# The pooled probabilities of batches 1 to 3, normalised block by block on ScalarE instead of at once on GpSimd

## The chip, the core and the metric

The kernel is one program on one core of a Trainium2 chip. A core has a matrix engine (TensorE, in the profile PE, its weight loads PEld), a vector engine (VectorE, DVE), an engine for functions and scaled copies (ScalarE, ACT), a general engine (GpSimd, POOL) that here also issues the accumulating DMAs, and SyncE (SP), which issues the other DMAs. Each engine runs its instructions strictly in order; semaphores tie the engines together. The metric is device time in microseconds, the median of three runs.

## The reference, cut to what matters

Three layers follow each other: an attention with a pooled and a local part, a channel mix, and a gated convolution. The part that the change touches is the softmax of the pooled attention.

```python
def sm_attn(qq, kk, vv):
    s = scale * np.matmul(qq, kk.transpose(0, 1, 3, 2))
    s = s - np.max(s, axis=-1, keepdims=True)
    a = np.exp(s)
    a = a / (np.sum(a, axis=-1, keepdims=True) + 1e-09)
    return np.matmul(a, vv)
q_d = q.reshape(B, H, Sd, factor, D).mean(axis=3)     # k_d, v_d likewise; Sd = 144
out_up = np.repeat(sm_attn(q_d, k_d, v_d), factor, axis=2)
...                                                   # out_local: 7 keys around each query
x = (out_up + out_local)                              # 4 batches, 8 heads of 64, 576 positions
x = _moe_ref(x, mu_k, mu_r, w_k, w_v, w_r)            # squared-relu channel mix, 512 -> 1024 -> 512
return _moe2_ref(x, w_in, conv_w, w_out)              # gate, 3-tap convolution, 512 -> 1024 -> 512
```

## The kernel before, in words

The attention of a batch is done for two groups of four heads (gp 0 and 1). A group consists of steps, each a function that issues a few instructions on one engine: the local scores (TensorE L504 and L513, then VectorE L530, L531, L542, L548 and ScalarE L539), the pooled scores (TensorE L575, 32 queries by 144 keys, so that 128 partitions hold a block of four heads and five blocks hold all queries), their softmax, then the way out: `down_out` transposes the pooled probabilities (L639), copies the transposes to SBUF on ScalarE (L647), multiplies by the pooled v (L662), copies again (L674, L676); `local_out` transposes the local probabilities (L694), copies (L699), multiplies (L713) and VectorE adds both parts (L728).

The pooled softmax runs like this: VectorE finds the maxima (L591, L592), ScalarE takes five exponentials with their sums (L598, one per block of 128 by 144), VectorE inverts the sums (L484, L485), and one engine multiplies the tile `pd` of 128 by 720 by the inverted sums (L610). For batch 0 that engine is VectorE, for batches 1 to 3 GpSimd: six instructions, one for each group of heads.

The channel mix of the batch before runs between these steps on TensorE: `up` (L869, L808 for the very first half batch) and `down` (L918, L836), in units of 12 matmuls (4 fp32 ones for L808 and L836). ScalarE and VectorE cut the weights, which arrive as fp64, into fp32 and then into two fp32r parts (L379, L380, L361, L364, L400 or L402, L406), and the activations likewise (L776 to L792, L888 to L906). The last third of the program is the gated convolution.

The order of each engine's instructions is not written by hand. `Program.order` is a list planner: every step has an engine (or a choice of engines), an estimated length and a list of keys that it reads and writes; from the back it works out a latest start for each step, shifted by a table of numbers per step (`EARLY`), and then fills the engines in planned time, each taking the ready step with the earliest latest start. Steps that may run on VectorE or ScalarE go to the one that the plan has free. A changed engine or length of one step therefore moves other steps as well, on every engine.

Of the kernel before, what the change touches and what calls it, by code (L numbers as in the profile page):

```python
# [14 lines left out]
AF = mybir.ActivationFunctionType  # L15
# [53 lines left out]
class Program:  # L69
# [15 lines left out]
    def step(self, engine, us, f, r=(), w=(), due=None, slack=1.0):  # L85
        n = len(self.steps)
        deps = set()
        for k in r:
            if k in self.writer:
                deps.add(self.writer[k])  # L90
        for k in w:
            deps.update(self.readers.pop(k, ()))
            if k in self.writer:
                deps.add(self.writer[k])
        for k in r:
            self.readers.setdefault(k, set()).add(n)
        for k in w:
            self.writer[k] = n
        deps.discard(n)
        self.steps.append((engine, us, f, due, slack))  # L100
        self.tags.append(self.tag)
        self.deps.append(deps)
        return n
# [95 lines left out]
def dve(n):  # L199
    return 0.13 + 1.1e-3 * n  # L200
# [19 lines left out]
def tile_local_attention__then__channel_mix__then__conv_glu(  # L220
# [16 lines left out]
    nc = tc.nc  # L237
# [8 lines left out]
    SD = S // FAC  # L246
# [11 lines left out]
    scale = 1.0 / math.sqrt(D)  # L258
# [82 lines left out]
    def ring(name, tiles, one=0):  # L341

        i = count[name] = count.get(name, -1) + 1
        i %= one or len(tiles)
        return tiles[i], (name, i)
# [68 lines left out]
    def group(b, gp):  # L414
# [7 lines left out]
        def tag(kind, i0):  # L422
            prog.tag = kind, b, gp, i0
# [58 lines left out]
        def inverse(rs, guard_scale):  # L482

            nc.vector.tensor_scalar(rs, rs, 1e-9, guard_scale, op0=ALU.add, op1=ALU.mult)  # L484
            nc.vector.reciprocal(rs, rs)  # L485
# [68 lines left out]
        def down_blocks(i0, i1):  # L554
            q0, m = i0 * PB, (i1 - i0) * PB
            qs = [min(q, q0 + m - BQ) for q in range(q0, q0 + m, BQ)]
            return q0, m, qs

        def down_scores(i0, i1):
            tag("ds", i0)  # L560
            q0, m, qs = down_blocks(i0, i1)
            nq = len(qs)
            pst, pk = ring("a2", a2_t)
            pd, pdk = ring("pd", pd_t, int(b > 0))
            sm, smk = ring("sums", sums)
            g["pd", i0] = (pd, pdk)
            mx, rs = sm[:, 0, 0:nq], sm[:, 1, 0:nq]
            sc = scale / FAC ** 2
            def f():
                for c in range(0, nq, 2):  # L570
                    for h in range(4):
                        for r in range(min(2, nq - c)):
                            q, at = qs[c + r], h ^ r
                            d, rows = g["kqd"][0][:, h // 2], slice(h % 2 * D, (h % 2 + 1) * D)
                            nc.tensor.matmul(  # L575
                                pst[at * BQ:(at + 1) * BQ, r, c // 2 * SD:(c // 2 + 1) * SD],
                                lhsT=d[rows, SD + q:SD + q + BQ], rhs=d[rows, 0:SD], start=True, stop=True,
                            )

            step(  # L580
                "PE", 0.2 * nq, f,
                [(g["kqd"][1], i, pr) for i in {0, i0} for pr in range(2)],
                [(pk, 0), (pk, 1)], slack=SL[i0 > 0],
            )
            for r in range(2):
                n_r = len(range(r, nq, 2))
                pv = pst[:, r, 0:n_r * SD].rearrange("p (c s) -> p c s", s=SD)

                def top(r=r, pv=pv):
                    m = mx[:, r:nq:2]  # L590
                    nc.vector.reduce_max(m, pv, axis=AX.X)  # L591
                    nc.vector.tensor_scalar_mul(m, m, -sc)  # L592

                step("DVE", 0.33 + 1.1e-3 * n_r * SD, top, [(pk, r)], [(smk, r)], slack=SL[i0 > 0])

                def ex(r=r, pv=pv):
                    for c in range(r, nq, 2):
                        nc.scalar.activation(  # L598
                            pd[:, c], pv[:, c // 2], AF.Exp, bias=mx[:, c:c + 1], scale=sc,
                            accum_out=rs[:, c:c + 1],  # L600
                        )

                step("ACT", 0.37 * n_r, ex, [(smk, r)], [(pk, r), (smk, "r", r), (pdk, r)], slack=SL[i0 > 0])
            step(
                "DVE", 0.4, lambda: inverse(rs, FAC), (), [(smk, "r", r) for r in range(2)], slack=SL[i0 > 0],
            )
            engine, us = ("DVE", dve) if b == 0 else ("POOL", pool)

            def norm(eng):
                eng.tensor_tensor(  # L610
                    out=pd[:, 0:nq], in0=pd[:, 0:nq], in1=rs.unsqueeze(2).to_broadcast([P, nq, SD]), op=ALU.mult
                )

            step(
                (engine,), (us(nq * SD),), norm, [(smk, "r", r) for r in range(2)],
                [(pdk, r) for r in range(2)], slack=SL[i0 > 0],
            )

# [61 lines left out]
        def local_out(i0, i1):  # L680
# [24 lines left out]
            for pr, hp in enumerate(pairs):  # L705
# [30 lines left out]
                step("DVE", 0.8, add, [odk], [(pk, 0), (pk, 1)] + ks, slack=SL[i0 > 0])  # L736

        return {"loads": loads, "kqd": pooled_kq, "s": local_scores, "ds": down_scores,
                "do": down_out, "lo": local_out}

# [663 lines left out]
```

## Time and profile before

| | |
|---|---|
| median of 3 runs | 584.84 us (584.05 to 585.73) |
| span of the profiled execution | 584.2 us, mean granted TensorE clock 0.991 |
| TensorE busy | 553.3 us (95%), weight loads 510.7 us |
| VectorE busy | 380.5 us (65%) |
| ScalarE busy | 329.3 us (56%) |
| GpSimd busy | 52.0 us (9%) |

The span runs from the first to the last instruction of one execution that the profiler recorded; the page gives no other time for that execution. A line of a timeline gives the start, the length from the first start to the last end of instructions of one form that follow each other, their number, and in brackets the idle time before them with what ended it. Instructions of one engine overlap at their edges, so that two starts are often closer than one length.

### The profile page before, as it was taken

Reading aid. Unit: us, or ns where it says so; the run is one execution under the profiler, and the core shown is the slowest. Engines: PE = TensorE matmul, PEld = TensorE weight load, DVE = VectorE, ACT = ScalarE, POOL = GpSimd, SP = SyncE. Lnnn points to the kernel's source line nnn. Section 1 sums busy time; section 2 is a strip of 40 time slices with the busy share of each in tenths; the row PEclk is TensorE's granted clock in tenths of the full one; section 3 lists DMA queues with packets and bytes.
Section 4 is the critical chain, followed back from the end, with each engine's and each line's share of the span. In section 5 each row is a group of like instructions: output and inputs, shape, how many; then the busy total and the mean of one; then the engine's idle time right before and its main releaser. Section 6 shows DMA issues by size and latency. Waiting matters only on the chain.

```text
span 584.2 us, 14308 instructions
## 1 busy us (share of the span) xinstructions
PE 553.3 (95%) x5900; PEld 510.7 (87%) x5900; DVE 380.5 (65%) x795; ACT 329.3 (56%) x779; POOL 52.0 (9%) x133
## 2 busy tenths in 40 slices
PE   4579979899999999999999999999999999999996
PEld 3457758789999999999999999899899898998995
DVE  6787698688534355344925899587586686395580
ACT  2458678576646475455838865455454455363441
POOL 3002021021121312110000000000000000000000
PEclk9999989898999999999999999999999999999999
DMA  9858998869467576712530530310400400100101
GB/s 262 292 191 216 296 293 209 283 181 302 141 136 207 113 220 160 171 51 76 187 116 2 202 110 0 123 42 0 146 18 1 145 19 1 54 2 1 54 2 54
DMA packets 42449, 74.14 MB, mean 127 GB/s; under 512 B 3648, under 2 KB 28736, under 8 KB 41472
## 3 DMA queue, kind: packets, MB, share of 16 engines
q1 hardware_dynamic: 38064, 65.27, 33.7%
q0 software_dynamic: 4320, 7.97, 8.9%
q8 instruction: 46, 0.75, 0.5%
q14 instruction: 19, 0.16, 0.1%
HBM read 59.06 MB, written 14.16 MB: 125 GB/s over the span
## 4 chain that ended last, share of the span: by engine, by line
PE 82%; DVE 7%; DMA 5%; ACT 3%; issue 2%; SPq 1%; ACTq 0%; POOL 0%; DVEq 0%
PE a L1301 17%; PE mm L869 15%; PE mm L918 15%; PE a L1221 8%; PE mm L1221 7%; PE mm L1180 4%; PE a L1180 4%; PE a L713 3%; DMA st_d<-in_moe_w_k 2%; DMA st_d<-in_moe_w_v 2%; PE a L694 2%; PE mm L836 2%; PE mm L808 1%; PE a L513 1%; PE a L639 1%
## 5 line engine op out<-in xcount | busy, mean ns | idle before, releaser
L1301 PE MATMUL a<-wk,wv 128*128 128x512 f32 x432 | 100.9, 390 | 0.0
L918 PE MATMUL mm<-k,wv 128*128 128x288 f32 x672 | 97.4, 301 | 0.2 <-ACT tmp L888 0.2
L1301 PEld LDWEIGHTS a<-wk,wv 128*128 128x128 f32 x432 | 80.9, 188 | 15.8
L869 PE MATMUL mm<-xk,wk 128*128 128x288 f32 x672 | 94.6, 299 | 0.0
L918 PEld LDWEIGHTS mm<-k,wv 128*128 128x128 f32 x672 | 91.9, 191 | 0.8 <-ACT tmp L888 0.5
L869 PEld LDWEIGHTS mm<-xk,wk 128*128 128x128 f32 x672 | 91.1, 191 | 1.1 <-issue 0.5
L1221 PE MATMUL mm<-k,wi 128*128 128x386 f32 x288 | 53.2, 338 | 0.4 <-ACT k L1205 0.3
L1221 PE MATMUL a<-k,wi 128*128 128x386 f32 x288 | 53.1, 338 | 0.0
L906 DVE TENSOR_TENSOR k<-tmp,k 128x288 fp32r<-128x288 f32 x56 | 25.7, 464 | 41.9 <-ACT k L899 41.2
L1221 PEld LDWEIGHTS mm<-k,wi 128*128 128x128 f32 x288 | 50.7, 188 | 1.5 <-ACT k L1205 0.7
L1221 PEld LDWEIGHTS a<-k,wi 128*128 128x128 f32 x288 | 50.8, 188 | 0.2
L728 DVE TENSOR_TENSOR xT<-a,od 128x288 f32<-128x288 f32 (+2 forms) x40 | 13.8, 392 | 37.6 <-PE a L713 37.6
L1276 ACT ACTIVATE tmp<-tmp 128x384 f32<-128x384 f32 x48 | 25.1, 523 | 21.6 <-DVE tmp L1270 21.6
L1266 DVE TENSOR_SCALAR tmp<-h,cw_sb 128x384 f32<-128x384 f32 x48 | 20.0, 417 | 25.6 <-ACT h L1251 12.2
L888 ACT ACTIVATE tmp<-mm 128x288 f32<-128x288 f32 x56 | 23.0, 412 | 22.3 <-PE mm L869 22.1
L1270 DVE SCALAR_TENSOR_TENSOR tmp<-h,cw_sb,tmp 128x384 f32<-128x384 f32 x48 | 29.7, 619 | 2.6
L1267 DVE SCALAR_TENSOR_TENSOR tmp<-h,cw_sb,tmp 128x384 f32<-128x384 f32 x48 | 29.7, 619 | 2.3
L1316 ACT ACTIVATE xT<-a 128x512 f32<-128x512 f32 x18 | 10.3, 597 | 36.2 <-PE a L1301 34.4
L1286 ACT CAST wv<-tmp 128x384 fp32r<-128x384 f32 x48 | 24.1, 511 | 9.3 <-DVE tmp L1279 9.2
L1279 DVE SCALAR_TENSOR_TENSOR tmp<-tmp,h 128x384 f32<-128x384 f32 x48 | 25.9, 553 | 3.0 <-ACT tmp L1276 2.5
L1288 DVE TENSOR_TENSOR wv<-tmp,wv 128x384 fp32r<-128x384 f32 x48 | 25.7, 553 | 2.9 <-ACT wv L1286 2.3
L361 DVE SCALAR_TENSOR_TENSOR st_f<-st_f,st_d 128x512 uint32<-128x512 uint32 x28 | 20.3, 725 | 11.1 <-ACT st_d L380 10.8
(149 smaller groups left out, 889.1 us busy)
## 6 DMA issues: line engine op xcount, KB each, us to landing
kq<-in_kq SPq DMA_DIRECT2D x12, 576.0 KB, 5.0
vw<-in_vw SPq DMA_DIRECT2D x6, 1152.0 KB, 9.5
kqd<-in_kqp POOLq DMA_DIRECT2D x18, 288.0 KB, 5.5
x_d<-xT SPq DMA_DIRECT2D x16, 288.0 KB, 7.0
v_d<-tmp SPq DMA_DIRECT2D x32, 144.0 KB, 4.0
out_dram<-xT SPq DMA_DIRECT2D x18, 256.0 KB, 2.0
st_d<-in_moe_w_k SPq DMA_DIRECT2D x8, 512.0 KB, 4.5
st_d<-in_moe_w_v SPq DMA_DIRECT2D x8, 512.0 KB, 5.4
```

The lines of the kernel that those rows point to most:

```text
L869: nc.tensor.matmul(pst[:, 0:NH], lhsT=wk_t[wt][:, kt, mt * P:(mt + 1) * P], rhs=xk[:, xs, kt, :], start=(kt == 0 and g == 0), stop=(kt == ...
L906: ("DVE",), (dve(NH),), lambda e, r=r, kh=kh, kl=kl: e.tensor_sub(kl, r, kh.bitcast(F32)),
L918: nc.tensor.matmul(pst[:, 0:NH], lhsT=wv_t[wt][:, kt, mt * P:(mt + 1) * P], rhs=xs, start=(kt == 0 and g == 0), stop=(kt == KF - 1 and g = ...
L1180: nc.tensor.matmul(pst[:, 0:CW], lhsT=late["wr"][wt][:, kt, mt * P:(mt + 1) * P], rhs=r_t[xs][:, kt, :], start=(kt == 0 and g == 0), stop= ...
L1221: nc.tensor.matmul(pst[:, 0:CW], lhsT=late["wi%d" % (mt * P // HF)][wt][:, kt, mt * P % HF:mt * P % HF + P], rhs=x1s[xs][:, kt, :], start= ...
L1267: nc.vector.scalar_tensor_tensor(out=cv, in0=tap(0), scalar=cw[:, 0, mt:mt + 1], in1=cv, op0=ALU.mult, op1=ALU.add)
L1270: nc.vector.scalar_tensor_tensor(out=cv, in0=tap(2), scalar=cw[:, 2, mt:mt + 1], in1=cv, op0=ALU.mult, op1=ALU.add)
L1276: step("ACT", act(CH), lambda: nc.scalar.activation(cv, cv, AF.Tanh, scale=0.5), (), [cvk])
L1279: lambda: nc.vector.scalar_tensor_tensor(out=gt, in0=cv, scalar=1.0, in1=tap(1), op0=ALU.add, op1=ALU.mult),
L1286: step("ACT", act(CH), lambda: nc.scalar.copy(gh, gf), ["wv_old", gk], [("gh", j)])
L1288: ("DVE",), (0.56,), lambda e: e.tensor_sub(gl, gf, gh.bitcast(F32)),
L1301: nc.tensor.matmul(pst, lhsT=xs[:, tt * P:(tt + 1) * P], rhs=wo[wt][:, kt, :], start=(kt == 0 and g == 0), stop=(kt == KF - 1 and g == 2),)
```

## The change

The planner's step for the normalisation of batches 1 to 3 is given to ScalarE with an estimated length of 0.3 us per block; the step issues five ACTIVATE instructions (Copy, scale taken per partition from the inverted sums of that block), where GpSimd issued one multiplication.

```diff
@@ -604,15 +604,19 @@
             step(
                 "DVE", 0.4, lambda: inverse(rs, FAC), (), [(smk, "r", r) for r in range(2)], slack=SL[i0 > 0],
             )
-            engine, us = ("DVE", dve) if b == 0 else ("POOL", pool)
+            engine, us = ("DVE", dve(nq * SD)) if b == 0 else ("ACT", 0.3 * nq)
 
             def norm(eng):
+                if eng is nc.scalar:
+                    for c in range(nq):
+                        eng.activation(pd[:, c], pd[:, c], AF.Copy, scale=rs[:, c:c + 1])
+                    return
                 eng.tensor_tensor(
                     out=pd[:, 0:nq], in0=pd[:, 0:nq], in1=rs.unsqueeze(2).to_broadcast([P, nq, SD]), op=ALU.mult
                 )
 
             step(
-                (engine,), (us(nq * SD),), norm, [(smk, "r", r) for r in range(2)],
+                (engine,), (us,), norm, [(smk, "r", r) for r in range(2)],
                 [(pdk, r) for r in range(2)], slack=SL[i0 > 0],
             )
 
```

Line numbers behind the change are larger by 4 (L639 is L643, L647 is L651, L662 is L666, L694 is L698, L713 is L717, L836 is L840, L853 is L857, L869 is L873, L918 is L922).

The planner's order changes from the first of the six normalisations on. On ScalarE, at batch 1, group 0, before (`pd` the pooled probabilities, `probs` the local ones, `pdt` the transposed pooled ones, `st_d` and `st_f` weights as loaded and as fp32, `mm` the sums of the channel mix in PSUM):

```order
L598 ACTIVATE pd_142,sums_148<-a_161,sums_148 128x144 x5
L379 ACTIVATE st_f_113<-st_d_110 128x512
L380 ACTIVATE st_d_110<-st_d_110 128x512
L400 CAST wv_117<-st_ff_152 128x4x128
L379 ACTIVATE st_f_114<-st_d_111 128x512
L380 ACTIVATE st_d_111<-st_d_111 128x512
L853 COPY tmp<-mm_156 128x288
L400 CAST wv_117<-st_f_113 128x4x128
L539 ACTIVATE probs_139<-probs_139 128x18x38
L647 COPY pdt_144<-a_158 72x2x128
L647 COPY pdt_144<-a_160 72x2x512
L853 COPY tmp<-mm_157 128x288
```

and now:

```order
L598 ACTIVATE pd_142,sums_148<-a_161,sums_148 128x144 x5
L379 ACTIVATE st_f_113<-st_d_110 128x512
L380 ACTIVATE st_d_110<-st_d_110 128x512
L400 CAST wv_117<-st_ff_152 128x4x128
L612 ACTIVATE pd_142<-pd_142,sums_148 128x144 x5
L379 ACTIVATE st_f_114<-st_d_111 128x512
L380 ACTIVATE st_d_111<-st_d_111 128x512
L539 ACTIVATE probs_139<-probs_139 128x18x38
L651 COPY pdt_144<-a_160 72x2x512
L651 COPY pdt_144<-a_158 72x2x128
L857 COPY tmp<-mm_156 128x288
L857 COPY tmp<-mm_157 128x288
```

The five scaled copies stand behind the cast that was there; the exponential of the local scores and the two copies of `pdt` now stand ahead of the two copies out of `mm`, and the cast of `st_f_113` has left ScalarE.

On TensorE in the same place, from the transposes of `pd` on, before:

```order
L639 MATMUL a_158<-ident,pd_142 72x128 x2
L639 MATMUL a_160<-ident,pd_142 72x128 x8
L836 MATMUL mm_156<-xT_120,st_f_113 128x288 x4
L662 MATMUL a_159<-pdt_144,vd_137 64x3x32 x4
L662 MATMUL a_159<-pdt_144,vd_137 64x2x32 x4
L662 MATMUL a_159<-pdt_144,vd_137 64x3x32 x4
L662 MATMUL a_159<-pdt_144,vd_137 64x2x32 x4
L694 MATMUL a_158<-ident,probs_139 128x128 x4
L836 MATMUL mm_156<-xT_120,st_f_114 128x288 x4
```

and now:

```order
L643 MATMUL a_158<-ident,pd_142 72x128 x2
L643 MATMUL a_160<-ident,pd_142 72x128 x8
L666 MATMUL a_159<-pdt_144,vd_137 64x3x32 x4
L666 MATMUL a_159<-pdt_144,vd_137 64x2x32 x4
L666 MATMUL a_159<-pdt_144,vd_137 64x3x32 x4
L666 MATMUL a_159<-pdt_144,vd_137 64x2x32 x4
L840 MATMUL mm_156<-xT_120,st_f_113 128x288 x4
L698 MATMUL a_158<-ident,probs_139 128x128 x4
L698 MATMUL a_159<-ident,probs_139 128x128 x4
L840 MATMUL mm_157<-xT_120,st_ff_151 128x288 x4
L698 MATMUL a_158<-ident,probs_139 128x128
L840 MATMUL mm_156<-xT_120,st_f_114 128x288 x4
```

The multiplication by the pooled v (L662, now L666) has moved ahead of the unit of the channel mix (L836, now L840) that stood between it and the transposes, and the local multiplication (L717) stands ahead of the last unit of L840.

On TensorE at the local scores of batch 2, group 0 (`a_160`, each run of L513 has eight rows in its second half), before:

```order
L513 MATMUL a_160<-kq_130 32x38 x4
L918 MATMUL mm_157<-k_123,wv_117 128x288
...
L869 MATMUL mm_156<-xk_122,wk_115 128x288
...
L575 MATMUL a_161<-kqd_133 32x144 x20
L513 MATMUL a_160<-kq_129 32x38 x4
L513 MATMUL a_160<-kq_130 32x38 x4
...
L918 MATMUL mm_156<-k_123,wv_117 128x288
```

and now:

```order
L513 MATMUL a_160<-kq_130 32x38 x4
L922 MATMUL mm_156<-k_123,wv_117 128x288
...
L922 MATMUL mm_156<-k_124,wv_117 128x288
L513 MATMUL a_160<-kq_129 32x38 x4
L513 MATMUL a_160<-kq_130 32x38 x4
...
L922 MATMUL mm_157<-k_123,wv_117 128x288
```

The second half of the scores was nine units of the channel mix behind the first, next to the pooled scores (L575); now one unit of 12 matmuls stands between the halves.

On GpSimd the six rows of L610 are gone and the accumulating DMAs (L356) keep their order but for one. From the pooled scores of batch 2, group 1, on, TensorE's order is as before.

## Rows read from the trace of the kernel before

**Rows 1.** The page: the busy line of TensorE, and the queue of instructions.

```profile
PE 553.3 (95%) x5900; PEld 510.7 (87%) x5900; DVE 380.5 (65%) x795; ACT 329.3 (56%) x779; POOL 52.0 (9%) x133
q8 instruction: 46, 0.75, 0.5%
```

**Rows 2.** Stretches: length, busy us of PE, PEld, DVE, ACT, POOL; clock, DMA share, GB/s.

```profile
77.00:140.00 63.00, 56.55 (x889) 50.16 (x888) 51.18 (x100) 45.32 (x103) 12.47 (x14) 0.92 0.84 242
140.00:327.00 187.00, 187.00 (x2598) 182.58 (x2597) 95.05 (x214) 114.86 (x289) 23.14 (x32) 1.00 0.52 143
327.00:360.00 33.00, 32.22 (x183) 31.12 (x182) 29.41 (x57) 21.55 (x45) 0.95 (x11) 1.00 0.25 84
```

**Rows 3.** Line L610: GpSimd's six normalisations (min/median/max ns), and who waited.

```profile
L610 POOL TENSOR_TENSOR pd<-pd,sums x6: 1384/1387/1731, 77.6 to 257.0; 128x720 f32<-128x720 f32 x6
  PEld a L639: 1.1, 1
```

**Rows 4.** Timeline of VectorE beside two normalisations: start, us, instruction, [idle before].

```profile
77.77 1.73 DVE L361 SCALAR_TENSOR_TENSOR st_f<-st_f,st_d 128x512 uint32<-128x512 uint32 x1 [0.35 <-ACT st_d L380]
79.53 0.69 DVE L364 SCALAR_TENSOR_TENSOR st_f<-st_d,st_f 128x512 uint32<-128x512 uint32 x1
80.68 0.51 DVE L531 TENSOR_TENSOR probs<-a,sums 128x342 f32<-128x342 f32 x1
117.18 1.88 DVE L406 TENSOR_TENSOR wr<-st_f,wr 128x512 fp32r<-128x512 f32 x1
```

**Rows 5.** ScalarE by form, 60 to 260 us: xcount | busy us, mean ns | idle before.

```profile
L380 ACT ACTIVATE st_d<-st_d 128x512 uint32<-128x512 uint32 x17 | 11.5, 676 | 0.0
L598 ACT ACTIVATE pd<-a,sums 128x144 f32<-128x144 f32 x30 | 11.0, 379 | 5.3 <-DVE sums L591 3.2 <-DVE sums L592 2.1
L776 ACT ACTIVATE tmp<-xT,mus 128x288 f32<-128x288 f32 x20 | 10.5, 533 | 10.7 <-DVE xT L728 10.7
L647 ACT COPY pdt<-a 72x1024 f32<-72x1024 f32 x5 | 5.1, 1011 | 3.6 <-PE a L639 3.4
L539 ACT ACTIVATE probs<-probs 128x684 f32<-128x684 f32 x5 | 3.9, 777 | 1.8 <-DVE probs L531 1.8
```

**Rows 6.** Timeline of ScalarE: the cast ahead of the first normalisation.

```profile
77.62 0.62 ACT L400 CAST wv<-st_ff 128x512 fp32r<-128x512 f32 x1
```

**Rows 7.** Timeline of TensorE behind the first normalisation.

```profile
79.00 0.41 PE L639 MATMUL a<-ident,pd 128*72 128x128 f32 x2 [0.61 <-POOL pd L610]
81.25 1.36 PE L639 MATMUL a<-ident,pd 128*72 128x128 f32 x8 [1.84 <-DVE probs L531]
82.41 3.54 PE L836 MATMUL mm<-xT,st_f 128*128 128x288 f32 x8
85.88 1.35 PE L662 MATMUL a<-pdt,vd 72*64 72x96 f32 x32
87.65 2.11 PE L836 MATMUL mm<-xT,st_f 128*128 128x288 f32 x8
```

**Rows 8.** Two of the stretches in which the granted clock was at half.

```profile
82.00:84.00 2.00, 2.00 (x7) 1.52 (x6) 1.93 (x5) 1.61 (x5) 0.42 (x1) 0.50 0.99 273
134.00:136.00 2.00, 2.00 (x10) 2.00 (x10) 1.56 (x3) 0.37 (x2) 0.85 (x1) 0.50 1.08 332
```

**Rows 9.** Timeline of TensorE, batch 1: waits for nothing shown, and for ScalarE.

```profile
105.50 0.37 PE L513 MATMUL a<-kq 64*32 64x38 f32 x31 [2.39 <-issue]
112.28 0.96 PE L575 MATMUL a<-kqd 64*32 64x144 f32 x40
127.31 0.82 PE L694 MATMUL a<-ident,probs 128*128 128x128 f32 x5 [0.90 <-ACT od L676]
132.44 0.30 PE L713 MATMUL a<-pt,vw 38*64 38x32 f32 x2 [0.50 <-issue]
```

**Rows 10.** Matmuls (PE x) and weight loads (PEld x) before and between two waits.

```profile
99.60:103.15 3.55, 3.52 (x131) 3.00 (x130) 3.21 (x9) 2.52 (x6) 0.00 (x0) 1.00 0.92 253
105.45:132.40 26.95, 25.32 (x384) 23.82 (x383) 21.68 (x42) 18.84 (x47) 4.93 (x5) 0.94 0.74 213
```

## The prediction

> **What bounds the kernel now.** I read the page first, then the busy time by stretch, then the timelines of the stretch that is not full. TensorE is busy for 553.3 of 584.2 us [rows 1]. The stretches show where the rest lies: from 140 to 327 us TensorE is busy for 187.00 of 187 us, from 327 to 360 it lacks 0.8, and from 77 to 140 it lacks 63 - 56.55 = 6.45 us at a mean granted clock of 0.92 [rows 2]. The six normalisations on GpSimd stand between 77 and 257 us, and TensorE waited for one of them, once, 1.1 us by its weight loads [rows 3]. So what the change does itself is small. It is worth what it does to the starved stretch from 77 to 140 us, and there it also moves other steps.
>
> Three things cost time in that stretch. First, plain waits: 0.61 for the normalisation and 1.84 us for VectorE at 81.25 [rows 7], and 0.90 for ScalarE at 127.31 [rows 9]. Second, two waits for nothing that the profile shows, 2.39 us at 105.50 in the local scores and 0.50 at 132.44 in the local multiplication [rows 9]. Third, stretches at the lower clock: in 82 to 84 and in 134 to 136 us the granted clock is 0.50, which is 1.2 GHz, each after TensorE had stood still [rows 7 to 9]; from the wait at 105.50 on it is 0.94 over 26.95 us, so that another 1.6 us are lost there [rows 10]. The unit of L836 at 82.41 took 3.54 us where the one at 87.65 took 2.11, so such a stretch costs about 1.4 us [rows 7].
>
> The second kind I read as TensorE's instructions arriving late. Between the two waits stand 384 + 383 = 767 matmuls and weight loads, to within one of 3 x 256; the instruction queue moved 46 packets, and 46 x 256 = 11776 is close to the 2 x 5900 of the kernel [rows 1, 10]. So instructions come in blocks of 256, and both waits stand at a block's end. The block before the 2.39 us wait was used up in about 3.55 us (131 + 130 instructions, the DMA engines 0.92 busy [rows 10]), because local scores are many short matmuls.
>
> **Weighed against the skill.** The Trainium skill, Runtime: NRT & Kernel Launch, Instruction fetch mechanics, says that instructions are fetched in blocks of 256 while the current block executes, and that crossing a block's end is "mostly hidden". The block size agrees with the 767 instructions between the waits; the 2.39 us do not agree with hidden. By that rule the second and the fourth term below would be nothing, and the sum +0.1 us, or 584.9; by the trace they are -1.2 and +1.0.
>
> **The change part by part.** The sum is made on the profiled span of 584.2 us and carried to the median of the runs, 584.84, which lies 0.6 us above it.
>
> *The normalisation itself.* Removed are six GpSimd instructions of 1.39 to 1.73 us [rows 3]; added are 6 x 5 scaled copies of 128 x 144. No row shows one. The exponentials of the same shape take 0.379 each, the scaled copies of twice the width (L776, scale per partition) 0.533 [rows 5]. That bounds five at 1.9 and 2.7 us if nothing overlaps; neighbours do overlap (the cast of 0.62 and its follower start closer than that [rows 6]), so the lower side is about 1.4. I take 1.7, nearest to the exponentials: as long as on GpSimd. VectorE wins, because an instruction beside the GpSimd multiplication stretched: 1.73 at 77.77 against 0.69 behind it, and 1.88 at 117.18 [rows 4]. That is 1.04 and about 1.2 us given back.
>
> *First term, batch 1 group 0.* Now the eight transposes start at 81.25, when VectorE's subtraction (80.68, 0.51) has emptied their PSUM tile [rows 4, 7]. Without the stretched instruction that is 80.2. The five copies start behind the cast, at 78.2, and end at 79.9 [rows 6]; so the two transposes at 79.00 slip to 79.9, the eight start at 80.2 and end near 81.5. But L666 (L662 before) now follows at once, and the copies that feed it stand on ScalarE behind two cuts of weights (2 x 0.68), the exponential (0.78) and their own 1.01 + 0.3 [rows 5]: 79.9 + 1.36 + 0.78 + 1.3 = 83.3, with overlaps 83.0. So TensorE idles 1.5 us there, does L666 by 84.4 and the unit by 86.5, against 87.2 before (85.88 + 1.35 [rows 7]): -0.7. But there are now two idle pieces of about 1.5 us, and if the slow clock follows as it did, 1.4 comes on top: +0.7. I take +0.3, nearer to the repeated slow stretch; bounds -0.7 and +2.1 (a full 0.533 per copy and a slow stretch).
>
> *Second term, the wait of 2.39 us.* The 256 instructions ahead of it are the same, in the same order. What changes is the traffic: the local multiplication stands one unit (2.1 us [rows 7]) earlier, so the loads that wait for it start up to 2 us earlier and are nearer their end when the block is fetched. I take half of the wait, -1.2. Bounds 0 and, with its slow stretch, -2.4 - 1.4 = -3.8.
>
> *Third term, batch 1 group 1.* From the pooled scores at 112.28 to the local multiplication stand as many units as before. The 0.90 at 127.31 [rows 9] goes, because the copies of the pooled result now stand ahead of the cuts that kept ScalarE. But the transposes come one unit sooner behind the pooled scores, and L666 waits for its copies behind the normalisation, +0.5. Sum -0.4; bounds -0.9 and +1.4.
>
> *Fourth term, the scores of batch 2 group 0.* One unit less (24 instructions) stands ahead of the local multiplication, so its block ends 20 instructions into the unit behind it, and the wait of 0.50 goes. The next block is the rest of that unit (4), the first half of the scores (168), a unit (24) and 60 instructions of the second half: the pattern that waited 2.39 us, and as quickly used up. Nothing in this trace says that it must wait; the nearest row is the 2.39, the other end 0. I take 1.5 and the same slow stretch as before, net +1.0. Bounds -0.5 - 1.4 = -1.9 and +1.9.
>
> *Fifth term, the other four normalisations.* TensorE's cover (187.00 of 187 us [rows 2]) hides them. In two places one unit less covers the chain from pooled scores to transposes; if that uncovers 0.5 us at each of four, 2 us. I take +0.2.
>
> *Elsewhere.* GpSimd's accumulating DMAs lose what stood in their way; nobody waited for them in the full stretch: 0. Behind 327 us no order changes, so whatever is won or lost by then is carried to the end.
>
> Sum: +0.3 - 1.2 - 0.4 + 1.0 + 0.2 = -0.1 us. Forecast **584.7 us**, no change; a measurement of this kernel can tell about 0.3%, or 1.75 us, from none.
>
> **The rivals.**
>
> *Faster: the starved stretch closes up.* The block at 105.50 comes in time, the clock stays up, and the new pattern doesn't wait: +0.3 - 3.8 - 0.4 - 1.9 + 0.2 = -5.6, or 579.2; with half of it 581.9. For it speaks that the loads start earlier and that VectorE gets 2.2 us back; against it that both patterns use a block up in 3.5 us with the DMA engines as busy as before.
>
> *Slower: instructions late twice.* The wait at 105.50 stays, and the split scores of batch 2 wait as long: +0.3 + 0 - 0.4 + 1.9 + 0.2 = +2.0, or 586.8, and 588.2 if a slow stretch is added. It decides if a block takes over 3.5 us to come, as the first did; against it speaks that the other halves in the full stretch did not wait.
>
> *Slower: ScalarE is the queue.* The copies of the transposes stand late behind copies and cuts in all six groups: +2.1 - 1.2 + 1.4 + 1.0 + 2.0 = +5.3, or 590.1; half of that is 587.5. For it speaks the 1.5 us worked out above and that ScalarE is busy 45.32 of 63 us in the starved stretch [rows 2]; against it the 61% in the full one.
>
> **How the numbers follow.** No change 0.39, the closing up 0.33, late instructions 0.16, ScalarE's queue 0.12. So faster 0.33, same 0.39, slower 0.28. The likeliest case alone spans 583.1 to 586.6. The range reaches into the others, to 580.2 and 588.2: most of the half-way closing up and both slower rivals at their half price; what lies beyond is the full closing up and the full queue, under 2 in 10.
>
> **What would show it.** Right: no GpSimd multiplication, no VectorE instruction stretched beside one, five ScalarE copies in 1.4 to 1.9 us; TensorE idle about 1.5 us ahead of L666 in batch 1 group 0 with half clock behind it; a shorter wait than 2.39 in the second half of the first scores; a wait for nothing shown about 30 matmuls into the second half of batch 2's; TensorE full from there to the convolution. Wrong: idle time of TensorE in 77 to 140 us that differs from 6.45 by more than 1.75 together with the slow stretches, or waits of TensorE for L612 in batches 2 and 3.

## The result, and the profile after

The changed kernel takes 590.25 us (median of 15 runs, 586.32 to 593.73), the kernel before 584.84 us beside it (15 runs, 580.72 to 589.76): ratio 1.0097, 95% interval 1.0072 to 1.0123. It is slower by about 5.4 us; the forecast was no change, and its range ended at 588.2. (A ratio and its interval are reckoned from the runs of both kernels; it need not be the quotient of the two medians.)

The profiled executions show little of that: spans of 585.7 and 584.2 us, and the one of after took 587.52 us in all, the second shortest of its 15. So the verdicts below rest on medians, and the profiles tell where time is lost, not how much a kernel loses on average.

The page of after, the lines that answer to [rows 1]:

```profile
PE 551.8 (94%) x5900; PEld 508.2 (87%) x5900; DVE 377.4 (64%) x800; ACT 335.3 (57%) x804; POOL 43.8 (7%) x127
q8 instruction: 46, 0.75, 0.5%
```

The stretches of [rows 2], now of after:

```profile
77.00:140.00 63.00, 54.76 (x947) 47.92 (x946) 50.05 (x103) 46.40 (x110) 9.75 (x12) 0.95 0.89 260
140.00:327.00 187.00, 186.78 (x2532) 181.47 (x2531) 92.02 (x213) 119.26 (x305) 17.55 (x28) 1.00 0.49 135
327.00:360.00 33.00, 32.23 (x184) 30.94 (x184) 29.20 (x55) 22.01 (x47) 0.95 (x11) 1.00 0.30 100
```

Behind 140 us next to nothing has changed: 186.78 of 187 us against 187.00. The starved stretch lacks 63 - 54.76 = 8.24 us in place of 6.45. TensorE's timeline in it shows the waits (answers to [rows 7, 9]):

```profile
80.14 1.47 PE L643 MATMUL a<-ident,pd 128*72 128x128 f32 x10 [1.42 <-ACT pd L612]
83.10 1.34 PE L666 MATMUL a<-pdt,vd 72*64 72x96 f32 x32 [1.50 <-ACT pdt L651]
84.38 3.90 PE L840 MATMUL mm<-xT,st_f 128*128 128x288 f32 x8
104.99 0.37 PE L513 MATMUL a<-kq 64*32 64x38 f32 x31 [0.98 <-issue]
118.45 1.35 PE L666 MATMUL a<-pdt,vd 72*64 72x96 f32 x32 [0.72 <-ACT pdt L651]
131.70 0.53 PE L922 MATMUL mm<-k,wv 128*128 128x288 f32 x2 [2.25 <-issue]
137.90 0.47 PE L513 MATMUL a<-kq 64*32 64x38 f32 x34 [1.16 <-issue]
```

Nearly every place is the forecast one: 1.5 us ahead of L666 and a slow unit behind it (3.90 us), a shorter wait in the second half of the first scores (0.98 for 2.39), a new one in the scores of batch 2 (1.16). One is not: the wait of 0.50 near 132 us, which was to go, is 2.25 us and now stands inside the unit of L922 behind the local multiplication. The granted clock is at half, 1.2 GHz, behind the waits at 83 and at 131.70 (clock in the third column from the right, as in [rows 8]):

```profile
84.50:87.80 3.30, 3.30 (x7) 2.37 (x8) 3.27 (x7) 2.25 (x6) 0.32 (x1) 0.50 0.96 269
132.30:135.50 3.20, 3.20 (x90) 2.85 (x89) 1.20 (x4) 0.03 (x1) 0.50 (x1) 0.50 1.03 405
```

The normalisation itself is as forecast: five scaled copies take 1.63 us, and VectorE's instruction beside them 0.69 where it took 1.73 [rows 4]. ScalarE and VectorE of after, timelines:

```profile
78.45 1.63 ACT L612 ACTIVATE pd<-pd,sums 128x144 f32<-128x144 f32 x5
81.79 1.26 ACT L651 COPY pdt<-a 72x1024 f32<-72x1024 f32 x2
```

```profile
78.09 0.69 DVE L361 SCALAR_TENSOR_TENSOR st_f<-st_f,st_d 128x512 uint32<-128x512 uint32 x1 [0.35 <-ACT st_d L380]
```

### The profile page after: what moved, and what is told of

It reads as the page before. It is cut to its first block, busy times and chain, and to the rows that moved or that the text cites. A ratio compares the mean times of both kernels' runs of the same rounds, so it can differ in the third digit from the quotient of the medians.

```text
span 585.7 us, 14319 instructions
## 1 busy us (share of the span) xinstructions
PE 551.8 (94%) x5900; PEld 508.2 (87%) x5900; DVE 377.4 (64%) x800; ACT 335.3 (57%) x804; POOL 43.8 (7%) x127
## 4 chain that ended last, share of the span: by engine, by line
PE 81%; DVE 6%; ACT 5%; DMA 5%; issue 2%; SPq 0%; ACTq 0%; POOL 0%
PE a L1305 17%; PE mm L922 15%; PE mm L873 14%; PE a L1225 8%; PE mm L1225 7%; PE a L1184 4%; PE mm L1184 4%; PE a L717 3%; DMA st_d<-in_moe_w_k 2%; DMA st_d<-in_moe_w_v 2%; PE mm L840 2%; PE a L698 2%; PE a L666 2%; PE a L513 1%; PE mm L812 1%
## 5 line engine op out<-in xcount | busy, mean ns | idle before, releaser
L922 PE MATMUL mm<-k,wv 128*128 128x288 f32 x672 | 97.3, 300 | 2.5 <-issue 2.3
L873 PE MATMUL mm<-xk,wk 128*128 128x288 f32 x672 | 94.1, 297 | 0.2 <-ACT tmp L892 0.2
L922 PEld LDWEIGHTS mm<-k,wv 128*128 128x128 f32 x672 | 91.3, 190 | 3.4 <-issue 2.5
L873 PEld LDWEIGHTS mm<-xk,wk 128*128 128x128 f32 x672 | 89.8, 188 | 2.1 <-issue 0.9
L857 ACT COPY tmp<-mm 128x288 f32<-128x288 f32 x32 | 12.7, 400 | 26.4 <-PE mm L922 20.8
```

Source lines behind the costliest of these rows:

```text
L873: nc.tensor.matmul(pst[:, 0:NH], lhsT=wk_t[wt][:, kt, mt * P:(mt + 1) * P], rhs=xk[:, xs, kt, :], start=(kt == 0 and g == 0), stop=(kt == ...
L922: nc.tensor.matmul(pst[:, 0:NH], lhsT=wv_t[wt][:, kt, mt * P:(mt + 1) * P], rhs=xs, start=(kt == 0 and g == 0), stop=(kt == KF - 1 and g = ...
```

## The experiments

The change does two things: another engine multiplies, and the planner, told so, moves the steps around it. Theory A: the new order costs the time, by the places at which TensorE's blocks of 256 instructions end and by its clock. Theory B: ScalarE, as a queue, costs it.

### The two halves, each alone

The first run gives the multiplication to ScalarE but lets the planner reckon with GpSimd, so that every engine's order is that of before. The second has the order of after, and GpSimd multiplies.

```diff
 # e1: the planner is told ("POOL", pool) as before; in norm:
+                if b:
+                    for c in range(nq):
+                        nc.scalar.activation(pd[:, c], pd[:, c], AF.Copy, scale=rs[:, c:c + 1])
+                    return
 # e2: the planner is told ("ACT", 0.3 * nq); in norm:
                 if eng is nc.scalar:
+                    eng = nc.gpsimd
```

> The planner still believes in a GpSimd step of 1.5 us, so that every engine's order is that of the kernel before; only the six multiplications are issued as 6 x 5 scaled copies on ScalarE. Theory A (the loss is the new order, because it sets where TensorE's blocks of 256 instructions end in fast stretches): as before, 583 to 586.5 us, ratio 0.998 to 1.003, the wait for nothing shown again behind 33 matmuls of the second half of the first scores and at the 142nd matmul of the local multiplication. Theory B (the loss is ScalarE as a queue, the copies and what stands behind them come late): 588 to 590 us, ratio 1.006 to 1.010, with waits of TensorE for L612-like copies and for the copies of the transposes.

> The planner believes in the ScalarE step, so that every engine's order is that of the changed kernel; the multiplication is issued on GpSimd as before. Theory A: as the changed kernel, 588.5 to 591.5 us, ratio 1.006 to 1.012, with the wait for nothing shown behind ten matmuls of the unit after the batch 1 local multiplication and behind 30 matmuls of the second half of batch 2's scores. Theory B: back to the kernel before, 583 to 586.5 us, ratio 0.998 to 1.003.

The engine alone: 584.1 us, ratio 0.9967 [0.9936, 0.9999]. The order alone: 592.8 us, ratio 1.0131 [1.0086, 1.0176], somewhat above what theory A gave it. Theory B falls: with neither order is ScalarE the slower engine; it is about 0.3% better than GpSimd (0.9967 to 1; 1.0097 to 1.0131), some 2 us, though the intervals hardly part the two. The order costs 1.3%, over 7 us. The waits of TensorE in the first (e1):

```profile
79.13 1.47 PE L643 MATMUL a<-ident,pd 128*72 128x128 f32 x10 [1.42 <-ACT pd L612]
103.79 0.51 PE L513 MATMUL a<-kq 64*32 64x38 f32 x31 [2.87 <-issue]
129.74 0.30 PE L717 MATMUL a<-pt,vw 38*64 38x32 f32 x2 [0.74 <-issue]
```

and in the second (e2; its L664 and L920 are L666 and L922 of after):

```profile
85.55 2.40 PE L664 MATMUL a<-pdt,vd 72*64 72x96 f32 x32 [1.37 <-ACT pdt L649]
110.11 0.37 PE L513 MATMUL a<-kq 64*32 64x38 f32 x31 [2.10 <-issue]
137.55 0.53 PE L920 MATMUL mm<-k,wv 128*128 128x288 f32 x2 [2.12 <-issue]
143.47 0.56 PE L513 MATMUL a<-kq 64*32 64x38 f32 x34 [2.13 <-issue]
```

The new order brings its waits along whichever engine multiplies. And the wait in the first scores is 2.10 us in e2, with the new order: that it was 0.98 in the profile of after belongs to that execution and is not shown for the order.

### The ends of the blocks moved

64 small products of zeros at the head of TensorE, where it waits for the first loads, move every end by 128 instructions (a product and a load each).

```diff
+    zero = const.tile([P, 32], BF16, name="zero")
+    nc.vector.memset(zero, 0.0)
+    for _ in range(64):
+        nc.tensor.matmul(a1_t[0][0:32, 0:32], lhsT=zero, rhs=zero, start=True, stop=True)
     prog.emit()
```

> The changed kernel with 64 small matmuls on zeros (128 instructions with their weight loads) at the head of TensorE's program, where TensorE waits anyway; they only shift by 128 instructions where blocks of 256 end. Theory A: the ends in the second half of the first scores, behind the batch 1 local multiplication and in the second half of batch 2's scores go; two short blocks of the three are gone and one remains (its end in the first half of batch 2's scores). 584 to 587.5 us, ratio to before 0.998 to 1.005, 3 to 6 us below the changed kernel; the three waits for nothing shown gone, one new wait possible in the first half of batch 2's scores. Theory B: 589.5 to 591 us, as the changed kernel.

> The kernel before with the same 64 small matmuls at the head. Theory A: both waits for nothing shown (2.39 us in the first scores, 0.50 in the local multiplication) go with the slow stretches behind them, 579.5 to 582.5 us, ratio 0.991 to 0.996. Theory B says nothing of it: instructions are not what is late, the waits stay where they are in the program, 584 to 586 us, ratio 0.999 to 1.002.

The changed kernel takes 588.06 us with them, ratio to before 1.0044 [1.0011, 1.0078]; the kernel before 581.86, ratio 0.9937 [0.9899, 0.9974]. Both gain 0.5 to 0.6%, some 3 us. The old waits between 95 and 140 us are gone and others have come, one of them in either kernel ahead of 15 us (2.46 us in e3, 0.63 in e4); from 60 us on these are left, of the changed kernel (e3):

```profile
72.53 0.59 PE L513 MATMUL a<-kq 64*32 64x38 f32 x43 [1.93 <-issue]
133.62 0.47 PE L513 MATMUL a<-kq 64*32 64x38 f32 x22 [2.69 <-issue]
```

and of before (e4):

```profile
72.85 0.59 PE L513 MATMUL a<-kq 64*32 64x38 f32 x43 [2.02 <-issue]
```

So where the ends fall is worth about 0.5% to either order. Between the two 6 us are left, though the changed one has the better engine. How much of that the ends still cost, this pair does not say: the new order has a wait of 2.69 us in the scores of batch 2 that the old one has not.

### The new order, place by place

The planner makes both orders; the head of the one is followed by the rest of the other, all with ScalarE's copies.

```diff
-        for i in self.order():
+        act = self.order(), self.start, self.chosen       # told ScalarE
+        ...                                               # pool: the same, told GpSimd
+        a, b = pool, act                                  # h3: act, pool
+        early = [i for i in a[0] if a[1][i] < 95.0]       # h2: 122.6 (planned time)
+        head = set(early)
+        for i in early + [i for i in b[0] if i not in head]:
         ...
```

> Scaled copies on ScalarE. The order is that of before through the pooled attention of batch 1, group 0 (until about 91 us), and the new one from there. Theory C (the loss sits in the second half of batch 2's scores, moved together ahead of the units of the first layer, with the block ends that fall into them): the idle of 1.5 us ahead of the pooled products goes, the fetch wait of 2.4 to 2.9 us near 104 us comes back, those near 130 us stay: 588 to 590 us, ratio 1.005 to 1.009. Theory D (the loss is the idle ahead of the pooled products of group 0 and the half clock behind it): 582 to 585, ratio 0.995 to 1.000. Theory E (the loss is in group 1 of batch 1): as C, 588 to 590.

> Scaled copies on ScalarE. The order is that of before through batch 1's attention (both groups, until about 123 us), and the new one from batch 2's scores on. Theory C: still slow, 588 to 591 us, ratio 1.005 to 1.010, with waits of 2 us and more for instructions in batch 2's scores, since the 256 instructions that end there take only an estimated 2.2 us (worked out from the durations of the same units) against 3.6 in the changed kernel. Theories D and E: 582 to 585, ratio 0.995 to 1.000.

> Scaled copies on ScalarE. The new order only through batch 1, group 0, that of before from there. Theory C: the idle of 1.5 us ahead of the pooled products and the short fetch wait near 104 us as in the changed kernel, none over 1 us near 130 us: 584 to 586 us, ratio 0.998 to 1.002. Theory D: 588 to 591, ratio 1.005 to 1.010. Theory E: 582 to 585.

| order of batch 1 gp 0 / batch 1 gp 1 / batch 2 on | median | ratio to before |
|---|---|---|
| new / new / new (after) | 590.25 us | 1.0097 [1.0072, 1.0123] |
| old / new / new (h1) | 590.31 us | 1.0061 [1.0028, 1.0094] |
| old / old / new (h2) | 587.61 us | 1.0018 [0.9988, 1.0048] |
| new / old / old (h3) | 585.64 us | 0.9982 [0.9956, 1.0008] |
| old / old / old (e1) | 584.1 us | 0.9967 [0.9936, 0.9999] |

The rows were measured beside different runs of before (medians of 584.84, 585.99 and 585.32 us), so the ratios are to be compared, not the medians. No theory wins: h1 fits C and E, h3 fits C, h2 lies between, and the waits of 2 us and more that C expected in h2's scores of batch 2 did not come. One place undone moves the ratio by 0.15 to 0.5% (gp 0: after to h1 and h3 to e1; gp 1: h1 to h2; batch 2 on: h2 to e1), no more than the width of an interval, so single steps are not told apart surely; that no one place holds the whole 1.3% is. The waits of h1 (here and in h2 and h3, L522, L677, L728, L851 and L933 are L513, L666, L717, L840 and L922 of after):

```profile
104.70 0.47 PE L522 MATMUL a<-kq 64*32 64x38 f32 x31 [3.12 <-issue]
119.69 1.35 PE L677 MATMUL a<-pdt,vd 72*64 72x96 f32 x32 [0.74 <-ACT pdt L662]
133.74 0.53 PE L933 MATMUL mm<-k,wv 128*128 128x288 f32 x2 [3.05 <-issue]
139.66 0.47 PE L522 MATMUL a<-kq 64*32 64x38 f32 x34 [0.74 <-issue]
```

of h2:

```profile
107.56 0.37 PE L522 MATMUL a<-kq 64*32 64x38 f32 x31 [2.44 <-issue]
133.50 0.30 PE L728 MATMUL a<-pt,vw 38*64 38x32 f32 x2 [0.67 <-issue]
```

and of h3:

```profile
82.39 1.34 PE L677 MATMUL a<-pdt,vd 72*64 72x96 f32 x32 [1.50 <-ACT pdt L662]
83.67 2.21 PE L851 MATMUL mm<-xT,st_f 128*128 128x288 f32 x8
103.89 0.37 PE L522 MATMUL a<-kq 64*32 64x38 f32 x31 [2.15 <-issue]
131.17 0.30 PE L728 MATMUL a<-pt,vw 38*64 38x32 f32 x2 [1.99 <-issue]
```

Read the units. With batch 1 gp 1 in the new order the end near 132 us falls into the unit of L922 behind the local multiplication (h1: 3.05 us), with the old one into the last two matmuls of that multiplication (h2: 0.67). The 1.50 us ahead of the pooled products comes and goes with gp 0: h1 and h2, where gp 0 is old, have at most 0.15 us there.

### ScalarE in the old order, with 64 products

> Every engine in before's order, the scaled copies on ScalarE, and 64 small products of zeros at the head of TensorE, which move the ends of its stretches of 256 instructions by 128. If the gain of ScalarE's copies at an unmoved order (ratio 0.9967) and that of the moved ends (0.9937) are separate: 579 to 582 us, ratio 0.988 to 0.993. If both come from the same wait: 582 to 584, ratio 0.993 to 0.997.

579.72 us, ratio 0.9891 [0.9847, 0.9934]: both gains add up, and this is the fastest kernel of the case, about 6 us below before beside it and, by the ratios, about 12 below after. Its waits for instructions from 60 us on:

```profile
71.26 0.59 PE L513 MATMUL a<-kq 64*32 64x38 f32 x43 [0.75 <-issue]
131.51 0.62 PE L513 MATMUL a<-kq 64*32 64x38 f32 x46 [1.79 <-issue]
```

### Two misses that found the place of the ends

I had estimated where the ends fall from the order of TensorE's instructions, and with 104 products (0.03 us each) expected fewer short blocks.

```diff
+    for _ in range(104):
+        nc.tensor.matmul(a1_t[0][0:32, 0:8], lhsT=zero, rhs=zero[:, 0:8], start=True, stop=True)
```

> The changed kernel with 104 small products of zeros at the head of TensorE: its stretches of 256 instructions end 208 earlier, so that between 75 and 140 us only one short one is left (in the first half of batch 2's scores, an estimated 3.5 us of work by the durations of its units). Theory F (waits at these ends and the half clock behind them are nearly all of what the new order costs): 580 to 584 us, ratio 0.990 to 0.997. Theory G (the idle in the exchange of batch 1, group 0, and the order of the units cost most, and waits for instructions only share the same idle): 586 to 589, ratio 1.001 to 1.006.

> Every engine in before's order, scaled copies on ScalarE, 104 small products of zeros at the head: between 75 and 140 us the shortest stretch of 256 instructions has an estimated 4.9 us of work, where 64 left one of about 2.0 us. If the waits at these ends set the time: no wait over 1 us is left between 90 and 140 us, 577 to 580 us, ratio 0.985 to 0.990. If they are hidden by now: as with 64, 579 to 581, ratio 0.988 to 0.992.

Both came out the other way: 596.61 us, ratio 1.0171 [1.0135, 1.0207], and 587.61, 1.0022 [0.9992, 1.0053]. The waits of the first:

```profile
109.03 0.27 PE L513 MATMUL a<-kq 64*32 64x38 f32 x7 [3.08 <-issue]
138.06 0.76 PE L513 MATMUL a<-kq 64*32 64x38 f32 x62 [2.24 <-issue]
143.98 0.28 PE L513 MATMUL a<-kq 64*32 64x38 f32 x10 [2.76 <-issue]
```

They are those of the unpadded kernel, 24 matmuls later in the program (31 left of the scores at 104.99 in after, 7 here): 208 instructions earlier is, by blocks of 256, 48 later. So I counted TensorE's records (matmuls, weight loads and the few semaphore and drain instructions among them) ahead of each of its waits of at least 0.5 us that end in "issue", in the twelve profiles up to then: 31 waits, and every one has 193 plus a multiple of 256 ahead of it (3009, 3777 and 4033 in after). My estimate of the ends had been off by about 63. Counted rightly, 40 products put no end into the scores of batch 2:

> The changed kernel with 40 small products of zeros at the head of TensorE. In the twelve profiles so far every wait for instructions from 60 us on has 193 plus a multiple of 256 TensorE records ahead of it, where the 256 records before took an estimated 5.2 us or less by the durations of their units. With 40 (80 records) no such end falls into the scores of batch 2 any more: waits are expected near 72 us (2 us) and perhaps in the local products (L717, up to 2 us in all). Theory F (those waits and the half clock behind them are nearly all that the new order costs): 581 to 584 us, ratio 0.991 to 0.997. Theory G (the idle in the exchange and the order of the units cost most of it): 586 to 589, ratio 1.000 to 1.006.

> Every engine in before's order, scaled copies on ScalarE, 40 small products of zeros at the head: waits for instructions near 72 us (2 us) and perhaps in the local products (up to 1.5 us), none in batch 2's scores over 1 us: 578 to 581 us, ratio 0.987 to 0.992. If what 64 gave was chance and not the place of the ends: 583 to 587, ratio 0.995 to 1.002.

The changed kernel takes 588.99 us so, ratio 1.0038 [1.0013, 1.0062], and before's order with ScalarE 581.8, 0.9924 [0.9893, 0.9956]. Theory F falls, G holds: the new order still costs 7.2 us. This pair can be accounted for, since its spans (586.0 and 578.8 us) differ by as much as its medians. TensorE's waits with the new order, two units beside them, and stretches at half clock:

```profile
73.72 0.32 PE L513 MATMUL a<-kq 64*32 64x38 f32 x19 [1.09 <-issue]
84.90 1.35 PE L666 MATMUL a<-pdt,vd 72*64 72x96 f32 x32 [1.49 <-ACT pdt L651]
86.17 3.89 PE L840 MATMUL mm<-xT,st_f 128*128 128x288 f32 x8
119.25 1.35 PE L666 MATMUL a<-pdt,vd 72*64 72x96 f32 x32 [0.73 <-ACT pdt L651]
134.00 2.77 PE L922 MATMUL mm<-k,wv 128*128 128x288 f32 x10 [1.83 <-issue]
```

```profile
86.20:89.60 3.40, 3.40 (x9) 2.49 (x8) 3.37 (x7) 2.38 (x6) 0.28 (x1) 0.50 0.97 257
134.00:137.40 3.40, 3.40 (x74) 3.12 (x74) 0.31 (x1) 0.60 (x2) 0.00 (x0) 0.50 0.99 373
77.00:140.00 63.00, 57.11 (x958) 49.94 (x957) 52.73 (x108) 48.50 (x121) 9.75 (x12) 0.95 0.92 263
```

and with the old:

```profile
73.51 0.33 PE L513 MATMUL a<-kq 64*32 64x38 f32 x19 [1.99 <-issue]
82.55 2.21 PE L840 MATMUL mm<-xT,st_f 128*128 128x288 f32 x8
84.90 1.34 PE L666 MATMUL a<-pdt,vd 72*64 72x96 f32 x32
118.79 1.35 PE L666 MATMUL a<-pdt,vd 72*64 72x96 f32 x32
```

```profile
77.00:140.00 63.00, 60.85 (x952) 54.69 (x951) 55.59 (x115) 54.12 (x133) 10.58 (x13) 1.00 0.94 269
```

In the old order a unit of L840 (82.55) stands between the transposes and L666, and the copies that L666 needs are made under it: no wait. In the new order that unit stands behind L666, so TensorE waits 1.49 us, and runs the unit at half clock, 3.89 us for 2.21. TensorE is busy 3.74 us less from 77 to 140 us (60.85 - 57.11), at a clock of 0.95 for 1.00 (63 x 0.05 = 3.2 us): 6.9 of the 7.2 us. By places: 1.49 ahead of the first L666, 0.73 ahead of the second, 1.83 for instructions, and two stretches at half clock, about 1.7 us each. So the wait for instructions and the half clock behind it are about half of the loss, and the missing cover ahead of L666 the other half.

Each pair of new and old order that has ScalarE and the same ends can be read so by place: the start of the matmul with the same number (from 0, dummies left out) in either profile, at numbers where both kernels have done the same products. What the new order loses (us, single executions):

| pair | gp 0 (1118 to 1193) | first scores (to 1617) | gp 1 (to 1728) | batch 2's scores (to 2204) | behind (to 2831) |
|---|---|---|---|---|---|
| after, e1 | +2.2 | -3.1 | +0.6 | +4.2 | -0.6 |
| 40 products: p3, p4 | +2.2 | +0.3 | +0.6 | +3.6 | -0.2 |
| 64 products: e3, b1 | +3.4 | +0.3 | +0.6 | +1.1 | -0.4 |
| 104 products: p1, p2 | +3.2 | +0.5 | +0.6 | +5.8 | -0.6 |

The two exchanges cost much the same in all four. In the first scores after waited 0.98 us where e1 waited 2.87 with half clock behind it; the other pairs have no such difference. The batch 2 column (it holds the unit of L922 behind the local multiplication too) changes most with the ends. The gain in the last column is a wait that ScalarE does cost, in the old order alone (e1):

```profile
187.69 1.86 PE L922 MATMUL mm<-k,wv 128*128 128x288 f32 x12 [1.01 <-ACT tmp L892]
```

## Why the prediction was wrong

**What failed.** The fourth term, the scores of batch 2, +1.0 with an upper bound of +1.9: "the wait of 0.50 goes". The block does end in the unit behind the local multiplication, as said, but TensorE waited there, 2.25 us in after, 2.12 in e2, 3.05 in h1. I had argued only that the unit covers it, without a row. And "the same slow stretch as before" took the half clock behind that wait as given; with the old order and ScalarE the profile shows none there (e1, clock 1.00 from 129.7 to 134 us). Over the place of this term, matmuls 1728 to 2204, after fell from 2.25 us ahead of before to 0.68 behind it, a loss of 2.9 us, and e2 lost 4.0 against before. Of after and of before, the lines in which these matmuls stand first:

```profile
125.63 2.30 PE L717 MATMUL a<-pt,vw 38*64 38x32 f32 x144
155.37 2.82 PE L922 MATMUL mm<-k,wv 128*128 128x288 f32 x20
```

```profile
127.88 1.83 PE L918 MATMUL mm<-k,wv 128*128 128x288 f32 x12
154.69 3.58 PE L918 MATMUL mm<-k,wv 128*128 128x288 f32 x25
```

In the chain of kernels the order from batch 2 on is 0.0051 of the ratio (h2 to e1), 3.0 us, without the wait in the unit of L922, which h2 has not.

**The second term**, -1.2: fell. The wait of 2.39 us was 0.98 in after's one profile, but 2.10 in e2 and 2.15 in h3, with the same units ahead of it, and 2.87 in e1 with the old ones. It differs from execution to execution; "the loads start earlier" was not shown.

**The third term**, -0.4: by place about right, after gained 0.6 us on before (matmuls 1617 to 1728), though not for the reason given. The 0.90 us for `od` that I booked as gain here is gone in e1 too: it belongs to the engine, and the order alone loses 0.6. Its 0.5 us ahead of L666 came (0.72). The step from h1 to h2, +2.5 us (0.0043), is past the bound of +1.4, but it holds the wait in the unit of L922 too, which the same reordering puts on the block's end near 132 us and which the prediction has in its fourth term.

**The first term**, +0.3: right in mechanism (idle 1.50, slow unit 3.90), and I weighed the slow stretch at half where it came in five of the six profiles with the new order at gp 0 (not in h3). By the ratios 0.9 to 2.1 us (h3 to e1, after to h1), by place 2.2 to 3.4 in the table; both are against kernels that have the engine's gain already, which the term counts in. Against before, as the term was reckoned, after lost 0.7 us (matmuls 1094 to 1193).

**The engine**: right. 1.63 us for five copies, no stretched VectorE instruction, about -2 us by itself.

**The fifth term and the rivals.** 186.78 of 187 us behind 140: with the new order the other normalisations stay hidden, +0.2 was enough. ScalarE as the queue is refuted as the cause (e1), though with the old order it does cost the 1.01 us at 187.69. Instructions late twice was the nearest rival: its mechanism is there, but with three waits in after, not two, and with the covers that the new order takes from L666 on top.

With the second term at nothing and the fourth at 2.9 to 4.0 the prediction's own sum gives +3.0 to +4.1, or 587.8 to 588.9 us; the rest of the measured 5.4 is not assigned to a place. The steps -1.9 (engine), +2.1, +2.5 and +3.0 (after to h1 to h2 to e1) add up to +5.7 us only because each is a difference of neighbouring ratios; each is uncertain by some 2.5 us. What is wait, half clock or idle is shown in full only for the pair with 40 products.

Why the same end waits 0.50 us in one kernel and 1.99 in another stays open in part. TensorE went on about 2.4 us behind the start of a packet of the instruction queue in both: in before the packet started at 130.00, 1.9 us ahead of the wait, in h3 at 128.79, 0.4 us ahead. Why it started so late is not shown.

## What to carry to other kernels

When a planner is told of a faster engine, time the engine and the order apart: here the engine won some 2 us and the order that came with it lost over 7. In a stretch where TensorE has little slack, look for the unit that covers the copies between transposes and their products, and keep it there. A wait of TensorE for nothing shown is worth counting: if the records between such waits are multiples of 256, a few dummy products at the head move them, to a better place or, as with 104 here, to a worse one.

## What the runs showed of the hardware

- All 36 waits of at least 0.5 us for instructions in the fourteen profiles stand at the same remainder, 193 of 256 records, and are 0.50 to 3.12 us long; 26 stand in the many short matmuls of the local scores (L513, or L522 in h1 to h3). In each of the 36, TensorE went on 2.20 to 2.82 us after a packet of the instruction queue (16384 bytes) had started, 1.22 to 1.59 after its end. The Trainium skill, Runtime: NRT & Kernel Launch, Instruction fetch mechanics, calls the crossing of such an end mostly hidden. By count the traces agree, two to four of these waits beside 46 or 47 packets of the instruction queue; by price they do not, since a kernel had up to 8.78 us of them (p1: 3.08 + 2.24 + 2.76, and 0.70 at 222.90 us).
- 80 or 128 small instructions at the idle head of TensorE made a kernel 0.4 to 0.8% faster, 208 made it 0.6 to 0.7% slower. For p1 its profile shows why (above); why p2 is slower than e1, with waits of 2.91 and 1.05 us for 2.87 and 0.74, is not settled.
- At gp 0 of batch 1 the half clock came with two idle pieces close together, but not always: behind 1.42 and 1.50 us (after), or 1.42 and 1.49 (p3), a unit of eight matmuls took 3.9 us; behind the same 1.42 and 1.50 in h3 it took 2.21, at a clock of 1.00 from 83.6 to 87 us. With only the first of the two (1.42 in e1, 1.30 in p4) it took 2.21 as well. What decided between after and h3 is not shown.
